# Split maxima turned into rows by two 64-row matmuls, a LayerNorm part on ScalarE, maxima 19 steps ahead

## The chip, the cores and the metric

The kernel runs on one core of a Trainium2 chip. The metric is the device time of one execution in microseconds (us). Before the change three runs took 1256.53, 1258.13 and 1259.32 us; the median is 1258.13. Engine names: PE is TensorE's matmul, PEld its weight load, DVE is VectorE, ACT ScalarE, POOL GpSimd, and SP is SyncE, which issues all the DMAs of this kernel.

## The reference

A pre-LayerNorm transformer block in float32: 2048 positions, width 448, 16 query heads of 28 columns that share one key and one value head, and a gated feed-forward part of 1792 columns.

```
h  = x + Attention(LN(x))      q = 16 heads x 28, k and v one head of 28
       p = softmax(q k^T * 28^-0.5);  (p v, heads side by side) @ wo
out = h + (silu(LN(h) @ w1) * (LN(h) @ w3)) @ w2
LN(x) = (x - mean) / sqrt(var + 1e-5), without gain or bias
```

## The kernel before

To keep float32 accuracy with fast matmuls, a value is split into a high part in the rounded type fp32r and a low part, the value minus the high part, and products are summed over high x high, low x high and high x low.

**Blocks and steps.** The queries are in 4 tiles of 512 (t) and 4 groups of 4 heads (g); one (t, g) is a block, i = 4t + g, 16 blocks. The attention loop (line 559) has 256 steps, 16 per block: step s = 16i + c treats key chunk c of 128 keys for block i. In a step, four `Head`s (line 269) each do two 64-row matmuls (key chunk as weights, QS[i] with 512 queries as the moving side), and ACT takes the exponential from PSUM (line 286). One step later `pv` (line 289) multiplies the exponentials with the values in four matmuls of 128 x 32 tiles, accumulated in a PSUM tile of its own (po).

**Maxima.** The softmax subtracts each row's true maximum. For that the scores are computed a second time, queries as weights and 512 keys as the moving side: a `Unit` (line 218) is one such matmul of 128 queries, 512 keys, one head, and a DVE maximum (line 236) of its 128x512 result. Each step has four units, for the block `AHEAD` = 20 steps on (`a_units`, line 349), so the last unit of block i is in step 16i-5. They come in pairs from heads that sit in the upper and lower 64 rows of QS. At the end of that step `max_done` (line 246) takes the maximum over the key tiles and negates it: nm, 128 queries x 16 columns. In the middle of step 16i-3 `max_rows` turns nm into 16 rows of 128 by one full transpose on PE (line 253), ACT copies the high part (line 255), and `max_low` subtracts it on DVE (line 260); then SP issues 8 DMAs (line 267) that put the rows into row 28 of each 32-row part of QS[i], where the keys' matrix holds ones. Thus the heads of block i, from step 16i on, add the negated maximum by the matmul itself.

**What sets the order.** Every engine executes in the order in which the program text issues: the schedule is manual. `at(s, fn)` (line 519) hangs a function on a step: a whole number is the end of the step, 0.4 and 0.5 its middle, before and after the maxima of the first two units are issued. In even steps the third and fourth head alternate with two units each, with PV between; in odd steps all four heads come first, then two units, PV, two units (lines 585 to 612). PSUM tiles other than po come from seven banks that are handed out as a ring (`bank`, `done`, lines 107 to 114): `bank` takes the one freed longest ago in program order, so a tile waits for the reader of the seventh tile before it.

**Second LayerNorm.** After a tile t is complete, in the blocks that follow, `wo_rows` (line 324) projects it and adds it to X, `ln_stats` and `ln_rstd` take mean, variance and the inverse root (a power on POOL, line 161), `ln_norm` (line 163) normalizes 128x448 on DVE, four per tile, and `ln_tr` transposes. For t = 0 and 1 this is done beside the attention steps (line 545), for t = 2 and 3 in the feed-forward part (line 671).

**Start.** Before the loop come the first LayerNorm, the projections and the splits of the weights (`split_wq`, lines 387 to 392, two of its subtractions on POOL), and, between projection matmuls, the units of block 0 and the first steps of block 1 in pairs (`both`, the list `first`, line 449).

Of the kernel before, what the change touches and what calls it, by code (L numbers as in the profile page):

```python
# [8 lines left out]
F32 = mybir.dt.float32  # L9
F32R = mybir.dt.float32r  # L10
AF = mybir.ActivationFunctionType
ALU = mybir.AluOpType
AX = mybir.AxisListType
# [3 lines left out]
P = 128  # L17
S = 2048
D = 448
# [3 lines left out]
T = 512  # L23
NT = S // T
NQ = T // P
NG = H // 4
NC = S // P
# [1 line left out]
NI = NT * NG  # L29
EPS = 1e-5  # L30
SCALE = DH ** -0.5
AHEAD = 20


@with_exitstack
def block_kernel(
# [13 lines left out]
    ve, se, ge, pe, sy = nc.vector, nc.scalar, nc.gpsimd, nc.tensor, nc.sync  # L50
# [4 lines left out]
    def f(ap):  # L55
        return ap.bitcast(F32)


    keep = ctx.enter_context(tc.tile_pool(name="keep", bufs=1))
    xt_pool = ctx.enter_context(tc.tile_pool(name="xt", bufs=2))  # L60
    ln_pool = ctx.enter_context(tc.tile_pool(name="ln", bufs=2))
    qs_pool = ctx.enter_context(tc.tile_pool(name="qs", bufs=3))
    wk_pool = ctx.enter_context(tc.tile_pool(name="work", bufs=2))
# [3 lines left out]

    X = [keep.tile([P, NQ, D], F32, name=f"X{t}") for t in range(NT)]
    ident = keep.tile([P, P], F32, name="ident")
    pexp = keep.tile([P, NQ], F32, name="pexp")  # L70
    KS = keep.tile([P, S], F32R, name="KS", tag="ks")
    VA = keep.tile([P, NC, 32], F32, name="VA")
# [34 lines left out]
    def bank(name="pb"):  # L107
        k = free.pop(0)
        ps = ps_w.tile([P, T], F32, name=name, tag=f"bank{k}")
        used[id(ps)] = ps, k  # L110
        return ps

    def done(ps):
        free.append(used.pop(id(ps))[1])
# [32 lines left out]
    LN = {}  # L147

    def ln_stats(t, n):
        if n == 0:  # L150
            LN[t] = (ln_pool.tile([P, NQ, 6], F32, name="st"),
                     ln_pool.tile([P, NQ, 2], F32, name="mv"),
                     ln_pool.tile([P, NQ], F32, name="rs"), {})
        st, mv, _, _ = LN[t]
        ve.bn_stats(st[:, n], X[t][:, n])
        ve.bn_aggr(mv[:, n], st[:, n])

    def ln_rstd(t, n0=0, n1=NQ):
        _, mv, rs, _ = LN[t]
        ve.tensor_scalar(rs[:, n0:n1], mv[:, n0:n1, 1], EPS, None, op0=ALU.add)  # L160
        ge.tensor_tensor(rs[:, n0:n1], rs[:, n0:n1], pexp[:, n0:n1], op=ALU.pow)

    def ln_norm(t, n):
        _, mv, rs, xns = LN[t]
        xn = xns[n] = ln_pool.tile([P, 512], F32, name="xn", bufs=4)
        ve.tensor_scalar(xn[:, :D], X[t][:, n], mv[:, n, 0:1], rs[:, n : n + 1],  # L166
                         op0=ALU.subtract, op1=ALU.mult)
        ge.tensor_copy(xn[:, D:], xn[:, 384:D])

    XT = {}  # L170
# [19 lines left out]
        done(last)  # L190


    MR = {}
    QS, MX, NM, PT, PO, WH, WS = {}, {}, {}, {}, {}, {}, {}

    def build_qs(i, ps=None):
        t, g = divmod(i, NG)
        st = wk_pool.tile([P, 2, T], F32R, name="qst")
        if ps is None:
            q = QR[t][:, g]  # L200
            se.activation(st[:, 0], q, AF.Copy)  # L201
            ge.tensor_tensor(st[:, 1], q, f(st[:, 0]), op=ALU.subtract)  # L202
        else:
            se.activation(st[:, 0], ps, AF.Copy)
            ve.tensor_tensor(st[:, 1], ps, f(st[:, 0]), op=ALU.subtract)


        QS[i] = qs_pool.tile([P, 4, T], F32R, name="qs")
        for p in range(2):
            for jj in range(2):  # L210
                for b in range(2):
                    r, j = 64 * jj + 32 * b, 2 * p + jj
                    sy.dma_start(f(QS[i][r : r + 32, 2 * p : 2 * p + 2]), f(st[32 * j : 32 * j + 32]))

    def rows(jj):
        return slice(64 * jj, 64 * jj + 64)

    class Unit:
# [7 lines left out]
        def mm(self):  # L226
            i, n, kt, r = self.i, self.n, self.kt, rows(self.jj)
            if i not in MX:
                MX[i] = wk_pool.tile([P, 16, 4], F32, name="mx")
            self.ps = bank("pa")  # L230
            pe.matmul(self.ps, QS[i][r, 2 * self.p, n * P : (n + 1) * P], KS[r, kt * T : (kt + 1) * T],  # L231
                      start=True, stop=True)

        def red(self):
# [9 lines left out]
            u.red()  # L244

    def max_done(i):
        NM[i] = wk_pool.tile([P, 16], F32, name="nm")
        ve.tensor_reduce(NM[i], MX[i], axis=AX.X, op=ALU.max, negate=True)  # L248

    def max_rows(i):  # L250

        ps = bank()
        pe.transpose(ps[:16, :P], NM[i], ident)  # L253
        mr = wk_pool.tile([16, 2, P], F32R, name="mr")
        se.activation(mr[:, 0], ps[:16, :P], AF.Copy)
        MR[i] = ps, mr

    def max_low(i):
        ps, mr = MR.pop(i)
        ve.tensor_tensor(mr[:, 1], ps[:16, :P], f(mr[:, 0]), op=ALU.subtract)  # L260
        done(ps)
        for k in range(2):
            for jj in range(2):
                r = 64 * jj + 32 * k + 28
                for p in range(2):
                    c = 8 * jj + 4 * p
                    sy.dma_start(f(QS[i][r : r + 1, 2 * p]).rearrange("o (n q) -> o n q", n=NQ), f(mr[c : c + 4, k]))  # L267

    class Head:

# [4 lines left out]
        def mm(self, k):  # L275
            i, c, (p, jj) = self.i, self.c, divmod(self.j, 2)
            if k == 0:
                self.ps = bank()
            r = rows(jj)
            pe.matmul(self.ps, KS[r, c * P : (c + 1) * P], QS[i][r, 2 * p + k], start=(k == 0), stop=(k == 1))  # L280

        def exp(self):
            i, c, (p, jj) = self.i, self.c, divmod(self.j, 2)
# [64 lines left out]

    def a_units(step):

        i, c = divmod(step, NC)
        if i >= NI:
            return None
        p, n = divmod(c // 2, NQ)
        us = [Unit(i, p, n, 2 * (c % 2) + k, jj) for jj in (1, 0) for k in range(2)]
        return us if c % 2 == 0 else [us[0], us[2], us[3], us[1]]


    for n in range(NQ):
        sy.dma_start(X[0][:, n], xv[0][:, n])  # L360
    make_identity(nc, ident)
    ge.memset(pexp, -0.5)

    with tc.tile_pool(name="start", bufs=1) as sp:
# [83 lines left out]

        first = [(both, 0, *divmod(pn, NQ), kt) for kt in range(4) for pn in range(8)]
        first.append((max_done, 0))  # L450
        for c in range(AHEAD - NC):
            first += [(both, 1, *divmod(c // 2, NQ), 2 * (c % 2) + k) for k in range(2)]
        first[-5:-5] = [(max_rows, 0), (max_low, 0)]

        def pairs(n=2):
            while n > 0 and first:
# [62 lines left out]
    def at(s, fn, *args):  # L519
        todo.setdefault(s, []).append((fn, args))  # L520
# [1 line left out]
    for g in range(NG):  # L522
        at(1 + 2 * g, split_wo, g)
    for i in range(1, NI):
        at(NC * i - 5, max_done, i)
        at(NC * i - 2.6, max_rows, i)
        at(NC * i - 2.5, max_low, i)
    for k in range(3, NI):
        at(NC * (k - 2) + 1, build_qs, k)
    LAST = NC * NI  # L530
    for i in range(NI - 1):
        e = NC * (i + 1)
# [3 lines left out]
    for t in range(NT - 1):  # L536
        e = NC * NG * (t + 1)
        for n in range(NQ):
            at(e + 14 + 2 * n, wo_rows, t, n)
            at(e + 14 + 2 * n, ln_stats, t, n)  # L540
        at(e + 22, ln_rstd, t)
        if t == NT - 2:
            continue
        for n in range(NQ):
            at(e + 23 + 2 * n, ln_norm, t, n)
        for c in range(4):
            at(e + 33.5 + 2 * c, lambda t, c: ln_tr(t, c, True), t, c)
    for t in range(NT):
# [5 lines left out]
    def run(s):  # L554
        for fn, args in todo.get(s, []):
            fn(*args)

    prev = None
    for s in range(LAST):
        i, c = divmod(s, NC)  # L560
        au = a_units(s + AHEAD)
        if s in (LAST - 6, LAST - 3):
            WH[0, (s - LAST + 6) // 3] = split_w((s - LAST + 6) // 3)
        if s == LAST - 2:
            WS[0, 0] = split_w2(0)
        hs = [Head(i, c, j) for j in range(4)]

        def pair(a, b):
            for k in range(2):
                a.mm(k)  # L570
                b.mm(k)
            a.exp()
            b.exp()

        def beside(h, us):
            for k in range(2):
                h.mm(k)
                us[k].mm()
            h.exp()

        def red(us):
            for u in us:
                u.red()

        pair(hs[0], hs[1])
        if au and c % 2 == 0:
            beside(hs[2], au[:2])
            run(s + 0.4)
            red(au[:2])
            run(s + 0.5)  # L590
            if prev is not None:
                pv(*prev)
            beside(hs[3], au[2:])
            red(au[2:])
        elif au:
            pair(hs[3], hs[2])
            for u in au[:2]:
                u.mm()
            run(s + 0.4)
            red(au[:2])  # L600
            run(s + 0.5)
            pv(*prev)
            for u in au[2:]:
                u.mm()
            red(au[2:])
        else:
            pair(hs[2], hs[3])
            run(s + 0.4)
            run(s + 0.5)
            pv(*prev)  # L610
        prev = (i, c)
        run(s)
# [120 lines left out]
```

## Time and profile before

| what | value |
|---|---|
| median of three runs | 1258.13 us |
| the profiled execution, its own time | 1257.51 us |
| its span, first to last instruction | 1255.7 us |
| mean granted TensorE clock | 0.997 of 2.4 GHz |
| busy: PE, DVE, ACT, POOL | 98%, 69%, 53%, 26% |
| attention loop, first PV matmul to last | 103.0 to 814.2 us |

In the profile an instruction stands under its source line; "out<-in" are tiles by name, "x8" a count. A wait is put down to the instruction that released it. A window's length is the difference of its two bounds, and a busy share of 1.00 under the clock is 2.4 GHz.

### The profile page before, as it was taken

To read this page: it belongs to the slowest core of one execution; us is meant where nothing else is said; L and a number is where in the kernel's file an instruction comes from. 1 tells how busy PE (TensorE), PEld (TensorE's weight loads), DVE (VectorE), ACT (ScalarE), POOL (GpSimd) and SP (SyncE) were. 2 spreads that over 40 slices of the span, in tenths; PEclk is the share of its full clock that TensorE was granted. 3 is DMA by queue.
4 is the path that set the end of the run, shared out by engine and by line. 5 is a ranking of instruction groups with operands and counts; after the bars stand their busy time and mean duration, and the time that the engine had idled before them with its cause. 6 is when DMAs were issued, how large, how long until landed. Compare 5 with 4: busy or idle time off the path is not lost.

```text
span 1255.7 us, 19960 instructions
## 1 busy us (share of the span) xinstructions
PE 1235.7 (98%) x7596; PEld 768.0 (61%) x7596; DVE 860.8 (69%) x1480; ACT 660.9 (53%) x1255; POOL 324.3 (26%) x240
## 2 busy tenths in 40 slices
PE   6999999999999999999999999999999999999998
PEld 4655444444544444544445543488888888888887
DVE  7998999999898999899998894033333334333333
ACT  3316878887688887688886687921111111211111
POOL 3201011101112101111110110344555445455551
PEclk9999999999999999999999999999999999999999
DMA  6220113110103110112110110023000000000000
GB/s 188 62 45 2 36 32 77 44 25 21 44 2 77 44 40 6 43 24 56 43 45 2 43 28 17 10 79 111 1 30 1 1 1 30 1 1 31 1 1 30
DMA packets 37960, 43.08 MB, mean 34 GB/s; under 512 B 12056, under 2 KB 30680, under 8 KB 37864
## 3 DMA queue, kind: packets, MB, share of 16 engines
q1 hardware_dynamic: 37864, 41.81, 12.8%
q8 instruction: 60, 0.98, 0.3%
q14 instruction: 36, 0.29, 0.1%
HBM read 20.25 MB, written 3.80 MB: 19 GB/s over the span
## 4 chain that ended last, share of the span: by engine, by line
PE 91%; DVE 6%; issue 1%; DMA 1%; POOL 0%; SPq 0%; ACT 0%; POOLq 0%
PE pa L127 23%; PE pb L280 21%; PE po L293 19%; PE pb L641 11%; PE pa L231 9%; DVE mx L236 5%; PE pb L127 4%; PE pa L330 3%; PE pb L179 1%; DMA qs<-mr 0%; PE pb L253 0%; DVE xn L166 0%; DVE nm L248 0%; SPq L267 0%; DMA X<-in_A_x_dram 0%
## 5 line engine op out<-in xcount | busy, mean ns | idle before, releaser
L236 DVE TENSOR_REDUCE mx<-pa 128x1 f32<-128x512 f32 x1024 | 635.9, 682 | 36.3 <-PE pa L231 14.8
L286 ACT ACTIVATE pt<-pb 128x512 f32<-128x512 f32 x1024 | 533.9, 601 | 153.9 <-PE pb L280 118.1
L280 PE MATMUL pb<-qs,KS 64*128 64x512 f32 x2048 | 358.2, 403 | 2.0 <-DMA qs<-mr 2.0
L280 PEld LDWEIGHTS pb<-qs,KS 64*128 64x128 f32 x2048 | 227.5, 185 | 159.8 <-DVE mx L236 80.5
L231 PE MATMUL pa<-KS,qs 64*128 64x512 f32 x1024 | 291.7, 441 | 0.9 <-ACT vt L425 0.9
L293 PE MATMUL po<-pt,VA 128*32 128x512 f32 x2048 | 274.4, 606 | 0.0
L127 PE MATMUL pa<-xh,qs 128*128 128x512 f32 x896 | 235.9, 395 | 0.0
L231 PEld LDWEIGHTS pa<-KS,qs 64*128 64x128 f32 x1024 | 133.7, 184 | 130.8 <-DVE mx L236 86.8
L127 PEld LDWEIGHTS pa<-xh,qs 128*128 128x128 f32 x896 | 167.8, 187 | 38.6 <-issue 0.8
L629 DVE TENSOR_TENSOR pt<-pa,pt 128x512 f32<-128x512 f32 x56 | 38.7, 691 | 222.7 <-PE pa L127 222.7
L641 PE MATMUL pb<-qst,pt 128*128 128x448 f32 x672 | 145.8, 367 | 0.0
L627 ACT ACTIVATE pt<-pa 128x512 f32<-128x512 f32 x56 | 33.5, 598 | 197.6 <-PE pa L127 197.5
L641 PEld LDWEIGHTS pb<-qst,pt 128*128 128x128 f32 x672 | 125.7, 188 | 12.5
L632 ACT ACTIVATE pt<-pt 128x512 fp32r<-128x512 f32 x56 | 35.4, 632 | 152.1 <-DVE pt L629 152.1
L202 POOL TENSOR_TENSOR qst<-QR,qst 128x512 fp32r<-128x512 f32 x15 | 19.3, 1285 | 314.7 <-ACT qst L201 314.7
L127 PE MATMUL pa<-xl,qs 128*128 128x512 f32 x336 | 96.4, 395 | 0.0
L293 PEld LDWEIGHTS po<-pt,VA 128*32 128x32 f32 x2048 | 40.9, 108 | 78.6 <-issue 72.0
L340 POOL TENSOR_TENSOR qs<-QR,qs 128x1024 fp32r<-128x1024 f32 x32 | 76.4, 2388 | 16.2 <-DVE qs L339 16.2
L317 POOL TENSOR_TENSOR OT<-OT,rb 128x512 f32<-128x512 f32 x16 | 20.8, 1298 | 201.3 <-PE pb L280 70.7
L127 PEld LDWEIGHTS pa<-xl,qs 128*128 128x128 f32 x336 | 62.9, 187 | 15.5
L633 DVE TENSOR_TENSOR pt<-pt 128x512 fp32r<-128x512 f32 x56 | 40.8, 728 | 39.1 <-ACT pt L632 39.1
L346 POOL TENSOR_TENSOR qst<-w_wo,qst 128x448 fp32r<-128x448 f32 x24 | 35.3, 1469 | 93.9 <-DVE qst L345 93.9
(80 smaller groups left out, 632.2 us busy)
## 6 DMA issues: line engine op xcount, KB each, us to landing
qs<-qst SPq DMA_DIRECT2D x128, 128.0 KB
rb<-sd SPq DMA_DIRECT2D x64, 64.0 KB
QR<-in_B_w_dram SPq DMA_DIRECT2D x16, 192.0 KB
X<-in_A_x_dram SPq DMA_DIRECT2D x3, 896.0 KB
out_dram<-X SPq DMA_DIRECT2D x3, 896.0 KB
qs<-mr SPq DMA_DIRECT2D x128, 2.0 KB
w<-in_B_w_dram SPq DMA_DIRECT2D x8, 192.0 KB
w_wo<-in_B_w_dram SPq DMA_DIRECT2D x6, 224.0 KB
```

What stands on the lines that cost most here:

```text
L127: pe.matmul(ps, lhs[b][:, cb, lsl], rhs[a][:, ca, rsl], start=(k == 0), stop=(k == len(terms) - 1),)
L231: pe.matmul(self.ps, QS[i][r, 2 * self.p, n * P : (n + 1) * P], KS[r, kt * T : (kt + 1) * T], start=True, stop=True)
L236: ve.tensor_reduce(MX[self.i][:, c, self.kt : self.kt + 1], self.ps, axis=AX.X, op=ALU.max)
L280: pe.matmul(self.ps, KS[r, c * P : (c + 1) * P], QS[i][r, 2 * p + k], start=(k == 0), stop=(k == 1))
L286: se.activation(f(PT[i, c, p][:, jj]), self.ps, AF.Exp, bias=0.0, scale=SCALE)
L293: pe.matmul(PO[i][32 * j : 32 * j + 32], VA[:, c], f(PT[i, c, j // 2][:, j % 2]), start=(c == 0), stop=(c == NC - 1))
L330: pe.matmul(ps, OS[a][:, g, n * P : (n + 1) * P], WO[b][:, g], start=(k == 0), stop=(k == 11))
L340: ge.tensor_tensor(wl, W13[k], f(wh), op=ALU.subtract)
L629: ve.tensor_tensor(sg, ps[1], sg, op=ALU.mult)
L632: se.activation(h[:, 0], sg, AF.Copy)
L633: ve.tensor_tensor(h[:, 1], sg, f(h[:, 0]), op=ALU.subtract)
L641: pe.matmul(Y[t][n][:, :D], hid[a][:, n * P : (n + 1) * P], w2s[:, b, :D], start=(k == 0 and m == 0), stop=(k == NF - 1 and m == 2))
```

## The change

- `AHEAD` is 19, so the last unit of block i is in step 16i-4, and two unit pairs fewer are computed at the start. `max_done` moves to the end of step 16i-4; `max_rows` stays in the middle of step 16i-3.
- `max_done` also splits: ACT copies the high part of nm into columns 0 to 15 of a zeroed 128x128 tile, POOL puts the low part into columns 16 to 31.
- `max_rows` makes two matmuls, one for each half of 64 queries, with the split tile as weights (64 rows, 128 columns) and a 64x64 identity as the moving side; each writes a PSUM tile of its own, and ACT copies 32x64 out of each. `max_low` is gone. Four DMAs of 4 KB replace eight of 2 KB; for that the four slots of QS are reordered.
- `ln_norm` in the attention loop runs on ACT, as scale and bias per row; `ln_rstd` gets two POOL operations of 128x4 for that bias wherever it treats a whole tile.

```diff
@@ -29,7 +29,7 @@
 NI = NT * NG
 EPS = 1e-5
 SCALE = DH ** -0.5
-AHEAD = 20
+AHEAD = 19
 
 
 @with_exitstack
@@ -67,6 +67,8 @@
 
     X = [keep.tile([P, NQ, D], F32, name=f"X{t}") for t in range(NT)]
     ident = keep.tile([P, P], F32, name="ident")
+    turn = keep.tile([P, 64], F32R, name="turn")
+    NEG = [keep.tile([P, P], F32R, name=f"neg{k}") for k in range(2)]
     pexp = keep.tile([P, NQ], F32, name="pexp")
     KS = keep.tile([P, S], F32R, name="KS", tag="ks")
     VA = keep.tile([P, NC, 32], F32, name="VA")
@@ -150,21 +152,27 @@
         if n == 0:
             LN[t] = (ln_pool.tile([P, NQ, 6], F32, name="st"),
                      ln_pool.tile([P, NQ, 2], F32, name="mv"),
-                     ln_pool.tile([P, NQ], F32, name="rs"), {})
-        st, mv, _, _ = LN[t]
+                     ln_pool.tile([P, NQ], F32, name="rs"), {}, ln_pool.tile([P, NQ], F32, name="nb"))
+        st, mv, _, _, _ = LN[t]
         ve.bn_stats(st[:, n], X[t][:, n])
         ve.bn_aggr(mv[:, n], st[:, n])
 
     def ln_rstd(t, n0=0, n1=NQ):
-        _, mv, rs, _ = LN[t]
+        _, mv, rs, _, nb = LN[t]
         ve.tensor_scalar(rs[:, n0:n1], mv[:, n0:n1, 1], EPS, None, op0=ALU.add)
         ge.tensor_tensor(rs[:, n0:n1], rs[:, n0:n1], pexp[:, n0:n1], op=ALU.pow)
-
-    def ln_norm(t, n):
-        _, mv, rs, xns = LN[t]
+        if n1 - n0 == NQ:
+            ge.tensor_tensor(nb, mv[:, :, 0], rs, op=ALU.mult)
+            ge.tensor_scalar(nb, nb, -1.0, None, op0=ALU.mult)
+
+    def ln_norm(t, n, act=False):
+        _, mv, rs, xns, nb = LN[t]
         xn = xns[n] = ln_pool.tile([P, 512], F32, name="xn", bufs=4)
-        ve.tensor_scalar(xn[:, :D], X[t][:, n], mv[:, n, 0:1], rs[:, n : n + 1],
-                         op0=ALU.subtract, op1=ALU.mult)
+        if act:
+            se.activation(xn[:, :D], X[t][:, n], AF.Identity, bias=nb[:, n : n + 1], scale=rs[:, n : n + 1])
+        else:
+            ve.tensor_scalar(xn[:, :D], X[t][:, n], mv[:, n, 0:1], rs[:, n : n + 1],
+                             op0=ALU.subtract, op1=ALU.mult)
         ge.tensor_copy(xn[:, D:], xn[:, 384:D])
 
     XT = {}
@@ -190,8 +198,7 @@
         done(last)
 
 
-    MR = {}
-    QS, MX, NM, PT, PO, WH, WS = {}, {}, {}, {}, {}, {}, {}
+    QS, MX, PT, PO, WH, WS = {}, {}, {}, {}, {}, {}
 
     def build_qs(i, ps=None):
         t, g = divmod(i, NG)
@@ -210,7 +217,7 @@
             for jj in range(2):
                 for b in range(2):
                     r, j = 64 * jj + 32 * b, 2 * p + jj
-                    sy.dma_start(f(QS[i][r : r + 32, 2 * p : 2 * p + 2]), f(st[32 * j : 32 * j + 32]))
+                    sy.dma_start(f(QS[i][r : r + 32, p::2]), f(st[32 * j : 32 * j + 32]))
 
     def rows(jj):
         return slice(64 * jj, 64 * jj + 64)
@@ -228,7 +235,7 @@
             if i not in MX:
                 MX[i] = wk_pool.tile([P, 16, 4], F32, name="mx")
             self.ps = bank("pa")
-            pe.matmul(self.ps, QS[i][r, 2 * self.p, n * P : (n + 1) * P], KS[r, kt * T : (kt + 1) * T],
+            pe.matmul(self.ps, QS[i][r, self.p, n * P : (n + 1) * P], KS[r, kt * T : (kt + 1) * T],
                       start=True, stop=True)
 
         def red(self):
@@ -244,27 +251,25 @@
             u.red()
 
     def max_done(i):
-        NM[i] = wk_pool.tile([P, 16], F32, name="nm")
-        ve.tensor_reduce(NM[i], MX[i], axis=AX.X, op=ALU.max, negate=True)
+
+        nm, neg = wk_pool.tile([P, 16], F32, name="nm"), NEG[i % 2]
+        ve.tensor_reduce(nm, MX[i], axis=AX.X, op=ALU.max, negate=True)
+        se.activation(neg[:, :16], nm, AF.Copy)
+        ge.tensor_tensor(neg[:, 16:32], nm, f(neg[:, :16]), op=ALU.subtract)
 
     def max_rows(i):
 
-        ps = bank()
-        pe.transpose(ps[:16, :P], NM[i], ident)
-        mr = wk_pool.tile([16, 2, P], F32R, name="mr")
-        se.activation(mr[:, 0], ps[:16, :P], AF.Copy)
-        MR[i] = ps, mr
-
-    def max_low(i):
-        ps, mr = MR.pop(i)
-        ve.tensor_tensor(mr[:, 1], ps[:16, :P], f(mr[:, 0]), op=ALU.subtract)
-        done(ps)
+        mr, ps = wk_pool.tile([32, P], F32R, name="mr"), [bank(), bank()]
+        for jj in range(2):
+            r = rows(jj)
+            pe.matmul(ps[jj][:, :64], NEG[i % 2][r], turn[r], start=True, stop=True)
+        for jj in range(2):
+            se.activation(mr[:, rows(jj)], ps[jj][:32, :64], AF.Copy)
+            done(ps[jj])
         for k in range(2):
             for jj in range(2):
-                r = 64 * jj + 32 * k + 28
-                for p in range(2):
-                    c = 8 * jj + 4 * p
-                    sy.dma_start(f(QS[i][r : r + 1, 2 * p]).rearrange("o (n q) -> o n q", n=NQ), f(mr[c : c + 4, k]))
+                r, c = 64 * jj + 32 * k + 28, 16 * k + 8 * jj
+                sy.dma_start(f(QS[i][r : r + 1, :2]).rearrange("o p (n q) -> o (p n) q", n=NQ), f(mr[c : c + 8]))
 
     class Head:
 
@@ -277,7 +282,7 @@
             if k == 0:
                 self.ps = bank()
             r = rows(jj)
-            pe.matmul(self.ps, KS[r, c * P : (c + 1) * P], QS[i][r, 2 * p + k], start=(k == 0), stop=(k == 1))
+            pe.matmul(self.ps, KS[r, c * P : (c + 1) * P], QS[i][r, 2 * k + p], start=(k == 0), stop=(k == 1))
 
         def exp(self):
             i, c, (p, jj) = self.i, self.c, divmod(self.j, 2)
@@ -348,17 +353,21 @@
 
     def a_units(step):
 
-        i, c = divmod(step, NC)
+        i, c = divmod(step + AHEAD, NC)
         if i >= NI:
             return None
         p, n = divmod(c // 2, NQ)
         us = [Unit(i, p, n, 2 * (c % 2) + k, jj) for jj in (1, 0) for k in range(2)]
-        return us if c % 2 == 0 else [us[0], us[2], us[3], us[1]]
+        return us if step % 2 == 0 else [us[0], us[2], us[3], us[1]]
 
 
     for n in range(NQ):
         sy.dma_start(X[0][:, n], xv[0][:, n])
     make_identity(nc, ident)
+    for jj in range(2):
+        ge.tensor_copy(turn[rows(jj)], ident[rows(jj), rows(jj)])
+    for w in NEG:
+        ge.memset(f(w), 0.0)
     ge.memset(pexp, -0.5)
 
     with tc.tile_pool(name="start", bufs=1) as sp:
@@ -450,7 +459,7 @@
         first.append((max_done, 0))
         for c in range(AHEAD - NC):
             first += [(both, 1, *divmod(c // 2, NQ), 2 * (c % 2) + k) for k in range(2)]
-        first[-5:-5] = [(max_rows, 0), (max_low, 0)]
+        first[-3:-3] = [(max_rows, 0)]
 
         def pairs(n=2):
             while n > 0 and first:
@@ -522,9 +531,8 @@
     for g in range(NG):
         at(1 + 2 * g, split_wo, g)
     for i in range(1, NI):
-        at(NC * i - 5, max_done, i)
-        at(NC * i - 2.6, max_rows, i)
-        at(NC * i - 2.5, max_low, i)
+        at(NC * i - 4, max_done, i)
+        at(NC * i - 2.5, max_rows, i)
     for k in range(3, NI):
         at(NC * (k - 2) + 1, build_qs, k)
     LAST = NC * NI
@@ -542,7 +550,7 @@
         if t == NT - 2:
             continue
         for n in range(NQ):
-            at(e + 23 + 2 * n, ln_norm, t, n)
+            at(e + 23 + 2 * n, ln_norm, t, n, True)
         for c in range(4):
             at(e + 33.5 + 2 * c, lambda t, c: ln_tr(t, c, True), t, c)
     for t in range(NT):
@@ -558,7 +566,7 @@
     prev = None
     for s in range(LAST):
         i, c = divmod(s, NC)
-        au = a_units(s + AHEAD)
+        au = a_units(s)
         if s in (LAST - 6, LAST - 3):
             WH[0, (s - LAST + 6) // 3] = split_w((s - LAST + 6) // 3)
         if s == LAST - 2:
```

## Rows read from the trace of the kernel before

**Rows 1.** The page: busy time of TensorE over the span, and the chain's shares.
```profile
PE 1235.7 (98%) x7596; PEld 768.0 (61%) x7596; DVE 860.8 (69%) x1480; ACT 660.9 (53%) x1255; POOL 324.3 (26%) x240
...
PE 91%; DVE 6%; issue 1%; DMA 1%; POOL 0%; SPq 0%; ACT 0%; POOLq 0%
```

**Rows 2.** Windows: stretch, length, busy (count) of PE, PEld, DVE, ACT, POOL, clock, DMA.
```profile
481.79:484.63 2.84, 2.84 (x25) 1.42 (x23) 2.84 (x5) 2.35 (x6) 0.00 (x0) 1.00 0.00 0
...
484.63:486.99 2.36, 2.36 (x21) 1.07 (x19) 2.13 (x5) 1.82 (x5) 0.00 (x0) 1.00 0.00 0
...
486.99:490.35 3.36, 3.25 (x26) 1.70 (x24) 3.33 (x7) 2.87 (x7) 0.00 (x0) 1.00 0.02 5
...
490.35:492.70 2.35, 2.35 (x19) 1.01 (x18) 2.03 (x5) 1.39 (x5) 0.00 (x0) 1.00 0.01 3
```

**Rows 3.** Timeline, 486.9 to 492.7 us: start, duration, engine, line, [idle before <-releaser].
```profile
487.48 0.22 DVE L248 TENSOR_REDUCE nm<-mx 128x16 f32<-128x64 f32 x1
...
487.62 3.67 DVE L236 TENSOR_REDUCE mx<-pa 128x1 f32<-128x512 f32 x6
...
491.47 0.28 DVE L260 TENSOR_TENSOR mr<-pb,mr 16x128 fp32r<-16x128 f32 x1 [0.19 <-ACT mr L255]
...
488.75 2.59 ACT L286 ACTIVATE pt<-pb 128x512 f32<-128x512 f32 x5 [0.49 <-PE pa L231]
...
491.19 0.25 ACT L255 ACTIVATE mr<-pb 16x128 fp32r<-16x128 f32 x1
...
489.47 0.56 PE L231 MATMUL pa<-KS,qs 64*128 64x512 f32 x2
...
490.35 1.06 PE L293 MATMUL po<-pt,VA 128*32 128x512 f32 x8
...
490.14 0.09 PEld L253 LDWEIGHTS pb<-ident,nm 128*16 128x16 f32 x1 [0.41 <-DVE mx L236]
```

**Rows 4.** Windows: intervals 15, into a block's first heads: first, last, sum of nine.
```profile
140.64:143.26 2.62, 2.62 (x20) 1.18 (x18) 2.39 (x5) 2.00 (x6) 0.00 (x0) 1.00 0.01 2
...
733.67:736.37 2.70, 2.70 (x21) 1.19 (x19) 2.47 (x5) 2.00 (x6) 0.00 (x0) 1.00 0.01 2
...
sum 25.10, PE 24.68 PEld 10.68 DVE 22.88 ACT 18.09 POOL 0.00; mean PE 2.74 PEld 1.19 DVE 2.54 ACT 2.01 POOL 0.00
```

**Rows 5.** Windows: intervals that hold a DVE normalization of the second LayerNorm.
```profile
344.96:348.11 3.15, 3.15 (x24) 1.66 (x22) 3.15 (x6) 2.66 (x6) 0.24 (x1) 1.00 0.00 0
...
355.97:359.76 3.79, 3.68 (x25) 1.59 (x23) 3.75 (x8) 3.30 (x8) 0.24 (x1) 1.00 0.00 0
```

**Rows 6.** Windows around the last block's start, and a later plain step.
```profile
767.57:769.89 2.32, 2.32 (x19) 0.92 (x17) 0.68 (x2) 2.27 (x6) 0.00 (x0) 1.00 0.00 0
...
774.16:779.09 4.93, 3.40 (x19) 1.14 (x17) 0.00 (x0) 2.99 (x7) 0.00 (x0) 0.87 0.01 3
...
779.09:782.17 3.08, 3.08 (x17) 0.96 (x16) 0.00 (x0) 1.75 (x4) 0.00 (x0) 0.66 0.00 0
...
796.05:798.18 2.13, 2.13 (x18) 0.83 (x20) 0.00 (x0) 2.07 (x5) 2.13 (x2) 1.00 0.00 0
```

**Rows 7.** Timeline there: SP's eight issues, and the weights that waited.
```profile
771.59 5.20 SPq L267 DMA_DIRECT2D qs<-mr  x8
...
777.25 0.30 PEld L280 LDWEIGHTS pb<-qs,KS 64*128 64x128 f32 x4 [1.07 <-DMA qs<-mr]
```

**Rows 8.** Lines by form, GpSimd: shapes, count, busy us, mean ns, idle before.
```profile
L202 POOL TENSOR_TENSOR qst<-QR,qst 128x512 fp32r<-128x512 f32 x15 | 19.3, 1285 | 314.7 <-ACT qst L201 314.7
...
L385 POOL TENSOR_TENSOR WKV<-wkv_r,WKV 128x384 fp32r<-128x384 f32 x1 | 1.0, 1001 | 0.5 <-ACT WKV L384 0.5
```

**Rows 9.** Timeline of the start: GpSimd, the weights waiting for it, one unit pair.
```profile
16.81 1.33 POOL L161 TENSOR_TENSOR rs<-rs,pexp 128x4 f32<-128x4 f32 x1 [5.66 <-DVE rs L160]
...
19.28 0.19 PEld L127 LDWEIGHTS pb<-xh,OS 128*128 128x128 f32 x1 [2.67 <-POOL OS L392]
...
95.92 0.50 PE L231 MATMUL pa<-KS,qs 64*128 64x512 f32 x2
```

## The prediction

> **What bounds the kernel now.** I read the page first: TensorE (PE) is busy in 98% of the span and carries 91% of the chain of waits [rows 1]. A busy PE is not a PE at its peak, so I then cut the attention loop into intervals. An interval runs from the weighted-value product (PV, line 293) of one step to that of the next, and I number it by its step in the block, 0 to 15. A plain even interval takes 2.84 us and a plain odd one 2.36 [rows 2], the first two windows: 5.20 for two steps. PE is busy all of it, VectorE (DVE) 4.97, ScalarE (ACT) 4.17, GpSimd (POOL) nothing, the clock is 1.00. The reader is to see that PE sets the pace in a plain step: DVE work that goes is worth nothing there unless PE waited for it. So I looked for intervals longer than plain ones; the change can only win or lose in these.
>
> Four kinds exist. Interval 12, where the maxima are turned into rows, takes 3.36 instead of 2.84 [rows 2]: 0.52 too long, in nearly every block. Interval 15, into the first heads of the next block, which need the rows by DMA, is too long in nine blocks: 25.10 in all [rows 4], less 9 x 2.36 = 3.9. The intervals with a DVE normalization are 3.15 instead of 2.84, and where it meets the maxima 3.79 instead of 3.36 [rows 5]. Around the last block four intervals lose several us [rows 6].
>
> The timeline of interval 12 says why it is long [rows 3]. The transpose's weights (line 253) start at 490.14, waiting for DVE. Seven PSUM banks go round as a ring, so its bank is that of the seventh tile before it: the last unit of the step before. That unit's max is the fourth of the six that start at 487.62, 0.60 apart ((3.67 - 0.68) / 5), so it ends at 487.62 + 1.80 + 0.68 = 490.10. PV follows 0.21 later, at 490.35. The negated maxima themselves (nm, line 248) were done at 487.70 and made nobody wait: they had a whole step.
>
> **The change, part by part.** *Maxima 19 ahead, the split on ACT and POOL: interval 12.* With 19 steps the last unit of a block is in step 16i-4, not 16i-5, so nm now comes behind that fourth max, while PE needs the split maxima where the transpose stood, half a step on. Walked through on [rows 3]:
> - Without nm in front of them the four maxima end some 0.25 earlier (nm's 0.22 and its hand-over): 489.85. nm then runs from 489.88 to 490.10.
> - ACT copies the high part. Its queue is in order: behind the fourth step-12 exponential (488.75 to 489.35) and ahead of step 13's first, which now starts at 489.27. The copy of 16 columns was never run here; the 16x128 copy of line 255 took 0.25, a 512 column exponential takes 0.60. Bounds 0.1 to 0.65, taken 0.20: 490.13 to 490.33.
> - POOL subtracts, 128x16. Subtractions of 512 and 384 columns take 1285 and 1001 ns [rows 8], 2.2 ns a column and 0.15 for none: 0.19 for 16. Bounds 0.1 and 1.3 (the 512 column row). Ready about 490.60.
> - The first small matmul could load at 490.60. The second takes the next bank of the ring, that of step 13's first head. Its exponential now starts behind the ACT copy, at 490.28, and ends at 490.88. So the second matmul goes at 490.93, and PV 0.2 later as behind the transpose: 491.14 instead of 490.35. The two matmuls are priced at that 0.2, bounds 0.05 and 0.5 (two unit matmuls after a change of tile, [rows 9]).
>
> Interval 12 grows by 0.79, to about 4.15. In interval 13 the next even step's first head takes the bank of step 13's last head, whose exponential ends at 490.28 + 3 x 0.49 + 0.60 = 492.35, against 491.14 + 1.10 = 492.24 when PE wants it: 0.14 more. Queued behind the waiting ACT copy are those four exponentials; behind the waiting matmul PV and the next two units, so DVE idles. PE has no slack in which to recover either. In 14 blocks 14 x 0.93 = +13.0.
>
> *What goes from DVE.* The subtraction of line 260 (0.28 and 0.19 idle) lies in an interval of 2.35, no longer than plain [rows 2]: worth nothing.
>
> *Four row DMAs for eight.* SP issues eight in 5.20, 0.65 each [rows 7]; the weights that wait for the seventh, issued at 771.59 + 6 x 0.65 = 775.5, start at 777.25: about 1.7 after its issue. Four issues from 492.6 (the two ACT copies behind step 13's exponentials) land by 492.6 + 1.95 + 1.7 = 496.3; the heads that want them come at 491.14 + 2.50 + 2.84 + 1.1 = 497.6. The excess of interval 15 goes: -3.9. What is late next is nothing, with 1.3 to spare.
>
> *LayerNorm on ACT.* Eight DVE normalizations go. Six cost 0.31 each, two 0.43 each [rows 5]: -2.7. ACT has 0.54 free in an odd interval [rows 2], and 448 columns take less than the exponential's 0.60 for 512: hidden. If that cover is gone it costs the difference. The Trainium skill (ScalarE: Activation LUTs, What ACT_TABLE_LOAD costs) gives 186 ns plus 0.833 ns a column and 93 ns more for each operand that is a pointer to a column; here scale and bias both are, so by it the operation would be 0.75, at most 0.2 over the gap eight times: an estimate of 1.6 less gain. No row here has an activation with two such operands.
>
> *Last block.* The five intervals from 767.57 to 782.17 took 14.60, with PE waiting for the rows and the clock at 0.87 and 0.66 [rows 6]. Now step 16i-4 has units, and no units follow: PV comes at about 490.9 on the scale above, an interval of 3.9; then 2.13, 2.13, 2.13 and some 2.6 (the output copy on ACT): 12.9, since the four DMAs just make it. -1.7, the extra step of units included.
>
> *Start.* Two unit pairs fewer. One took up to 0.50 on PE [rows 9], one rode beside another: between 0 and 1.0, taken -0.65. Against this POOL gets two 128x4 operations between the power at 16.81 and the weight splits at 18.11, for which PE waited 2.67 [rows 9]: about 0.2 each, bounds 0.1 and 1.3, +0.4. Together -0.25.
>
> *Rows of QS reordered, padding, the ident copies:* the loads of QS come twelve steps before use, and POOL is idle then; nothing.
>
> Sum: 13.0 - 3.9 - 2.7 - 1.7 - 0.25 = +4.5. The profiled execution took 1257.5 (span 1255.7, and 1.8 around it), so 1262.0; it lies 0.6 under the median of 1258.1.
>
> **The rivals.** *A, the wait is hidden.* If what makes interval 12 long is mostly the transpose's own change of tile, two matmuls in the units' 64-row tiles bring it to about 2.95, -0.4 in 14 blocks, nothing in interval 13, and the last block gains 3.5: -5.7 - 3.9 - 2.7 - 3.5 - 0.25 = -16, 1241. In favour: PEld waits 0.41 there and the transpose alone stands in 16-column tiles. Against: the bank's max ended at 490.10 and the transpose went 0.04 later, so a wait, not the tile, set it; and nm now comes after that same max. It decides if the split maxima are ready by 489.9, 0.7 sooner than I find. The Trainium skill (TensorEngine Tiling (Array Packing), Key Properties) says that changing the tiling mode drains the engine, which speaks for this rival; the 0.21 from the transpose to PV is all that the rows leave for it. *A', half of the wait hidden* (DVE further ahead than walked): +0.25 in 14 blocks, -8.5 for the rest: -5, 1252.5.
>
> *B, POOL is dear.* If the small subtraction costs 1.0 instead of 0.19, as the 128x4 power with 1.33 suggests [rows 9], PV slips to 491.6, interval 13 is plain: 14 x 1.25 - 8.5 = +9, 1266.5. If the clock fell after the new waits as it did in the last block, it would be more: an interval at 0.66 took 3.08 [rows 6], some 0.9 over plain; in 14 blocks +12 beside my +4.5, 1274. Against the latter: two idles of 0.78 and 0.75 led to that fall, mine are near 0.7 alone.
>
> *C, no change that can be told.* The chain costs 0.6 a block, not 0.93 (a shorter copy, interval 13 untouched): 8.4 - 8.5 = 0, 1257.5.
>
> **How the numbers follow.** A measurement of this kernel can tell about 0.2%, 2.5 us. My forecast, 1259 to 1265, has 0.54, of which 0.06 falls within 0.2%; B 0.14; C 0.12; A 0.08; A' 0.12. So faster 0.20, same 0.18, slower 0.62. The likeliest has 1262.0, own range 1259 to 1265. From 1250 to 1270 takes in A', C, the forecast and the first of B, and leaves out A and the clock's case (0.04).
>
> **What would show it.** Interval 12 at 4.1 in the changed trace, ACT idle for 0.7 before the 128x16 copy with DVE's nm as releaser, small matmuls waiting for ACT or POOL, interval 13 at 2.5, interval 15 at 2.36, normalization intervals at 2.84, no DMA wait at the last block. If interval 12 is at or under 3.4, the forecast is wrong, and the time is near 1245.

## Result, and the profile after

The changed kernel takes 1263.52 us (median of 6 runs, 1262.65 to 1264.20) against 1257.94 (6 runs) of the kernel before on the same chip: ratio 1.0043, 95% interval 1.0030 to 1.0056, 5.6 us slower. The forecast was 1262.0, own range 1259 to 1265. The profiled execution took 1262.77, with a span of 1260.8 instead of 1255.7.

The page of the changed kernel, busy time by engine and the chain of waits by engine:

```profile
PE 1231.3 (98%) x7612; PEld 769.3 (61%) x7612; DVE 852.1 (68%) x1456; ACT 668.3 (53%) x1295; POOL 333.5 (26%) x274
...
PE 83%; issue 8%; DVE 5%; POOL 2%; SPq 1%; DMA 1%; ACT 1%; POOLq 0%; DVEq 0%; ACTq 0%
```

PE is busy for 4.4 us less than in [rows 1] in a span that is 5.1 longer: it waits more. The windows of the changed kernel, columns as in [rows 2], show where. In order: intervals 12 and 13 of the block of [rows 2], an interval 15, the first and the second normalization interval of a tile, and around the last block's start intervals 12, 13, 15 and 0.

```profile
490.43:494.61 4.18, 3.38 (x26) 1.83 (x24) 4.07 (x8) 2.83 (x7) 0.22 (x1) 1.00 0.01 4
494.61:496.97 2.36, 2.36 (x19) 1.01 (x18) 1.02 (x3) 1.66 (x6) 0.00 (x0) 1.00 0.00 0
...
227.55:229.91 2.36, 2.36 (x21) 1.02 (x19) 2.13 (x5) 1.81 (x5) 0.00 (x0) 1.00 0.00 0
348.02:351.13 3.11, 3.11 (x25) 1.54 (x23) 2.85 (x5) 3.04 (x7) 0.24 (x1) 1.00 0.00 0
353.48:356.32 2.84, 2.84 (x25) 1.39 (x23) 2.84 (x5) 2.35 (x6) 0.00 (x0) 1.00 0.02 6
...
773.71:777.72 4.01, 2.89 (x25) 1.40 (x23) 3.07 (x6) 2.67 (x7) 0.22 (x1) 1.00 0.00 0
777.72:779.84 2.12, 2.12 (x18) 0.82 (x17) 0.00 (x0) 1.84 (x6) 0.00 (x0) 1.00 0.00 0
781.97:784.45 2.48, 2.48 (x18) 1.06 (x16) 0.00 (x0) 2.26 (x6) 0.00 (x0) 1.00 0.02 3
784.45:786.58 2.13, 2.13 (x18) 0.83 (x18) 0.00 (x0) 2.13 (x6) 0.00 (x0) 1.00 0.00 0
```

Interval 12 went from 3.36 to 4.18, with PE idle for 0.80 of it; interval 13 is plain; interval 15 fell to plain; the normalization intervals fell to plain but for the first of each tile; the last block's wait [rows 6] is nearly gone, and the clock stays at 1.00 there. The timeline of that interval 12, which answers to [rows 3] (start, duration, engine, line):

```profile
493.39 0.22 DVE L256 TENSOR_REDUCE nm<-mx 128x16 f32<-128x64 f32 x1
...
493.64 0.22 ACT L257 ACTIVATE neg<-nm 128x16 fp32r<-128x16 f32 x1 [0.86 <-DVE nm L256]
493.76 2.04 ACT L291 ACTIVATE pt<-pb 128x512 f32<-128x512 f32 x4
...
493.93 0.22 POOL L258 TENSOR_TENSOR neg<-nm,neg 128x16 fp32r<-128x16 f32 x1 [13.31 <-ACT neg L257]
...
494.20 0.37 PEld L265 LDWEIGHTS pb<-turn,neg 64*128 64x128 f32 x2 [1.12 <-POOL neg L258]
494.61 0.16 PEld L298 LDWEIGHTS po<-pt,VA 128*32 128x32 f32 x8
...
496.14 0.69 DVE L243 TENSOR_REDUCE mx<-pa 128x1 f32<-128x512 f32 x1 [1.34 <-PE pa L238]
```

It is the walk of the prediction, link by link: nm behind the last maximum, then ACT, which has stood idle for 0.86 with step 13's exponentials queued behind the copy, then POOL, then the weights, which waited; and DVE, which everyone waited for, idles for 1.34 afterwards because the next units come late.

Two more lines of the changed kernel are needed below: the normalization on ACT, from the view by form (count, busy us, mean ns, idle before), and POOL's weight splits at the start, from the timeline.

```profile
L172 ACT ACTIVATE xn<-X,nb,rs 128x448 f32<-128x448 f32 x8 | 6.1, 768 | 0.7 <-POOL nb L166 0.7
```

```profile
18.81 2.58 POOL L401 TENSOR_TENSOR OS<-OT,OS 128x448 fp32r<-128x448 f32 x2
```

### The profile page after: what moved, and what is told of

It reads as the page before. It is cut to its first block, busy times and chain, and to the rows that moved or that the text cites. A ratio compares the mean times of both kernels' runs of the same rounds, so it can differ in the third digit from the quotient of the medians.

```text
span 1260.8 us, 19897 instructions
## 1 busy us (share of the span) xinstructions
PE 1231.3 (98%) x7612; PEld 769.3 (61%) x7612; DVE 852.1 (68%) x1456; ACT 668.3 (53%) x1295; POOL 333.5 (26%) x274
## 4 chain that ended last, share of the span: by engine, by line
PE 83%; issue 8%; DVE 5%; POOL 2%; SPq 1%; DMA 1%; ACT 1%; POOLq 0%; DVEq 0%; ACTq 0%
PE pa L129 23%; PE pb L285 18%; PE po L298 16%; PE pb L649 11%; PE pa L238 6%; PE pb L129 4%; DVE mx L243 3%; PE pa L335 3%; PE pb L187 1%; SPq L220 1%; PE pb L265 1%; POOL OS L327 0%; DVE st L157 0%; DMA rb<-sd 0%; POOL OT L322 0%
## 5 line engine op out<-in xcount | busy, mean ns | idle before, releaser
L285 PE MATMUL pb<-qs,KS 64*128 64x512 f32 x2048 | 354.6, 401 | 0.0
L258 POOL TENSOR_TENSOR neg<-nm,neg 128x16 fp32r<-128x16 f32 x16 | 3.5, 222 | 216.3 <-ACT neg L257 216.3
```

## The experiments

All ratios are against the kernel before, run beside. Line numbers in a fence are of the kernel it is from; the cuts of code show the lines that matter, and "..." stands for lines left out. "The loop" is the time from the first PV matmul to the first of the PV in step 255, the last step; it is 709.0 in the kernel before and 713.3 in the changed one.

**The normalization on ACT alone.** The kernel before with only this part; of its edit the one line that moves the operation:

```diff
-            at(e + 23 + 2 * n, ln_norm, t, n)
+            at(e + 23 + 2 * n, ln_norm, t, n, True)
```

> The kernel before with the second LayerNorm's normalization (t = 0 and 1) on ACT, and nothing else of the change. The changed kernel's trace: six of the eight normalization intervals fall by 0.31 to 0.43 us, the first of each tile (3.15) stays. Theory of parts that add up: -2.0 in the loop, +0.4 or nothing at the start (two POOL operations before the weight splits), so 1256.0 to 1256.5, ratio 0.9987. Rival, the operations with two column pointers (0.76 us) delay the exponentials and with them PE: no gain, ratio 1.000 or over.

Measured: 1258.39 (11 runs), ratio 1.0003 (0.9994 to 1.0011): no change. The rival's result, but not for its reason. The normalization intervals did fall, and part of the gain was given back at the next block's first heads, whose row DMAs were already late. The first two windows are a normalization interval (3.15 before) and interval 14 of the first such block, the third the same block's interval 15, which was a plain 2.35 before:

```profile
352.47:355.31 2.84, 2.84 (x24) 1.40 (x22) 2.84 (x5) 2.35 (x6) 0.00 (x0) 1.00 0.03 6
363.38:366.23 2.85, 2.85 (x25) 1.39 (x23) 2.85 (x5) 2.36 (x6) 0.00 (x0) 1.00 0.02 4
366.23:368.93 2.70, 2.70 (x20) 1.18 (x19) 2.48 (x5) 1.99 (x6) 0.00 (x0) 1.00 0.01 2
```

Of 2.1 won in six intervals of two tiles 0.7 went this way. In the profiled execution the loop is still 1.8 shorter than before; but the first PV comes 2.1 later, at 105.0, and the part behind the loop is 0.6 longer. The start varies by as much between executions (last section), so what the two POOL operations add to it is not shown by the total.

**Four row DMAs alone.** The kernel before with QS reordered, and:

```diff
-                for p in range(2):
-                    c = 8 * jj + 4 * p
-                    sy.dma_start(f(QS[i][r : r + 1, 2 * p])..., f(mr[c : c + 4, k]))
+                c = 8 * jj
+                sy.dma_start(f(QS[i][r : r + 1, :2])..., f(mr[c : c + 8, k]))
```

> The kernel before with the four slots of QS reordered and four row DMAs of 4 KB in place of eight of 2 KB, and nothing else. Theory: intervals 15 fall to 2.36 in all blocks (-3.9 in nine) and the wait at the last block, its two long intervals and the fall of the clock go (-3.4): about 1250.5, ratio 0.994. Interval 12 stays at 3.36. Rival, the maxima in rows are late by themselves and not by the number of issues: intervals 15 stay at 2.6 to 3.1 and the time at 1258.

Measured: 1251.68, ratio 0.9950 (0.9935 to 0.9965). At the last block, where [rows 6] has 4.93 and 3.08 with the clock at 0.87 and 0.66, and in an interval 12:

```profile
485.27:488.65 3.38, 3.27 (x26) 1.72 (x24) 3.35 (x7) 2.89 (x7) 0.00 (x0) 1.00 0.02 5
771.12:773.81 2.69, 2.58 (x19) 1.06 (x17) 0.00 (x0) 2.27 (x6) 0.00 (x0) 1.00 0.01 3
773.81:775.94 2.13, 2.13 (x18) 0.83 (x17) 0.00 (x0) 2.13 (x6) 0.00 (x0) 1.00 0.00 0
```

The number of issues on SP was the cause of the late rows, and this part alone is worth 6 us (7.5 in the loop of the profiled execution, whose first PV came 1.2 later than in the kernel before). So the rest of the change costs about 12.

**The split on DVE.** The changed kernel, with

```diff
-        se.activation(neg[:, :16], nm, AF.Copy)
-        ge.tensor_tensor(neg[:, 16:32], nm, f(neg[:, :16]), op=ALU.subtract)
+        ve.tensor_copy(neg[:, :16], nm)
+        ve.tensor_tensor(neg[:, 16:32], nm, f(neg[:, :16]), op=ALU.subtract)
```

> The changed kernel with both halves of the split on DVE (two 128x16 operations) in place of the copy on ACT and the subtraction on POOL. ACT's queue no longer holds an operation that waits for DVE; the chain behind the last maximum stays in being, nm and two more DVE operations. Theory, the chain behind the last maximum sets interval 12: the small matmuls start about 0.1 sooner and the second no longer waits for step 13's first exponential, interval 12 goes from 4.19 to about 3.9: -0.3 in 15 blocks, -4.5, 1259. Rival, ACT's queue alone is the cost: interval 12 at 3.2 or less, 1248. Rival, the two matmuls are dear by themselves: 4.19 and 1263.5 as in the changed kernel.

Measured: 1258.10 (10 runs), ratio 1.0006 (0.9997 to 1.0015). Interval 12 is 3.81; the chain on DVE, and the weights that wait for it:

```profile
490.83 0.22 DVE L256 TENSOR_REDUCE nm<-mx 128x16 f32<-128x64 f32 x1
491.08 0.17 DVE L257 CAST neg<-nm 128x16 fp32r<-128x16 f32 x1
491.29 0.17 DVE L258 TENSOR_TENSOR neg<-nm,neg 128x16 fp32r<-128x16 f32 x1
...
491.52 0.18 PEld L265 LDWEIGHTS pb<-turn,neg 64*128 64x128 f32 x2 [0.91 <-DVE neg L258]
```

The chain behind the last maximum is the main part of the wait. The way over ACT and POOL had added 0.37 of 4.18: from the end of nm to the first weights it is 0.47 here and 0.60 there, and both weights load at once here, where the second had come 0.19 later, behind the exponential that ACT's copy had held up.

**Twenty steps ahead again.** The changed kernel, with the split at the end of step 16i-5:

```diff
-AHEAD = 19
+AHEAD = 20
...
-        at(NC * i - 4, max_done, i)
+        at(NC * i - 5, max_done, i)
```

> The changed kernel with the maxima 20 steps ahead again and max_done, with its split on ACT and POOL, at the end of step 16i-5: the split has a whole step more before PE needs it. Theory, only the lead time was short: interval 12 at 3.2 to 3.36 (the bank of the seventh tile before), -0.9 in 15 blocks, 1250. Rival, the copy in ACT's queue costs wherever it stands right behind a last maximum: it would now hold up the exponentials of step 12 by about 1.0 us (they are due 0.8 before nm ends), PE would wait for their banks, interval 11 or 12 together would be some 0.7 to 1.0 over plain, and the time 1257 to 1263.

Measured: 1262.91, ratio 1.0041 (1.0028 to 1.0055): the rival. The split is ready at 492.90, two us before PE loads it, and interval 12 is still 4.03. On ACT the copy waits 1.69 for nm, ahead of exponentials that are due, and PE then waits three times for the bank of one:

```profile
492.39 0.22 ACT L257 ACTIVATE neg<-nm 128x16 fp32r<-128x16 f32 x1 [1.69 <-DVE nm L256]
492.51 2.04 ACT L291 ACTIVATE pt<-pb 128x512 f32<-128x512 f32 x4
```

```profile
493.14 0.18 PEld L238 LDWEIGHTS pa<-KS,qs 64*128 64x128 f32 x1 [0.28 <-ACT pt L291]
493.62 0.18 PEld L285 LDWEIGHTS pb<-qs,KS 64*128 64x128 f32 x1 [0.30 <-ACT pt L291]
494.11 0.75 PEld L285 LDWEIGHTS pb<-qs,KS 64*128 64x128 f32 x7 [0.30 <-ACT pt L291]
```

So lead time is not enough: two things are wrong, the lead and the copy's place in ACT's queue.

**The small matmuls behind PV.** The changed kernel, with a hook behind PV in odd steps:

```diff
-        at(NC * i - 2.5, max_rows, i)
+        at(NC * i - 3 + 0.6, max_rows, i)
...
             pv(*prev)
+            run(s + 0.6)
```

> The changed kernel with the two small matmuls and what follows them moved behind PV in step 16i-3 (one PV, 1.0 us, later); the split stays on ACT and POOL at the end of step 16i-4. Theory: PE no longer waits for the split, since PV now covers the chain, so interval 12 falls from 4.19 to 2.85; but the copy still holds the four exponentials of step 13 by about 0.8, and the two unit matmuls behind the small ones, and the next step's first head, take the banks of those exponentials: interval 13 grows from 2.36 to about 3.2. Together -0.5 in 15 blocks: 1256. Rival, ACT's queue has slack enough: interval 13 at 2.5, 1246. Rival, PE waits as long as before, only behind PV: 1263.

Measured: 1262.97, ratio 1.0038 (1.0024 to 1.0052): no gain. Interval 12 is 2.91, as the theory has it, but interval 13 is 3.64, not 3.2. The small matmuls start at once behind PV now, and behind them PE's weights wait three times 0.30 for an exponential of step 13. The theory had a wait of 0.8 on a plain interval; it left out that the small matmuls take time of their own: without the waits this interval is 2.61, as the next kernel shows.

```profile
495.66 0.18 PEld L238 LDWEIGHTS pa<-KS,qs 64*128 64x128 f32 x1 [0.30 <-ACT pt L291]
496.15 0.18 PEld L238 LDWEIGHTS pa<-KS,qs 64*128 64x128 f32 x1 [0.30 <-ACT pt L291]
...
496.63 0.53 PEld L285 LDWEIGHTS pb<-qs,KS 64*128 64x128 f32 x5 [0.30 <-ACT pt L291]
```

```profile
491.21:494.12 2.91, 2.91 (x25) 1.47 (x23) 2.85 (x5) 1.87 (x4) 0.00 (x0) 1.00 0.00 0
494.12:497.76 3.64, 3.45 (x21) 1.44 (x20) 2.79 (x6) 2.63 (x8) 0.22 (x1) 1.00 0.00 0
...
sum 6.55, PE 6.36 PEld 2.90 DVE 5.65 ACT 4.50 POOL 0.22; mean PE 3.18 PEld 1.45 DVE 2.82 ACT 2.25 POOL 0.11
```

The two intervals have the same sum as in the changed kernel, 4.18 + 2.36 = 6.54: moving the matmuls alone moves PE's wait and does not shorten it, since the exponentials come as late as before.

**Both together.** The split on DVE and the small matmuls behind PV.

> The changed kernel with the split on DVE and the small matmuls behind PV. Theory: no exponential waits for a maximum, the split ends under PV (it ended 0.3 after PE was ready for PV in the kernel with the split alone on DVE): interval 12 at 2.85, interval 13 at about 2.5 for the two matmuls, together -0.8 in 15 blocks against the split on DVE alone, 1246, ratio 0.990. Rival, the two more DVE operations make DVE the later engine: interval 14 longer, 1250 or over.

Measured: 1248.58, ratio 0.9925 (0.9910 to 0.9939). Each edit alone left the kernel at 1258 and 1263; together they remove both waits, 2.91 + 2.61 = 5.52:

```profile
483.25:486.16 2.91, 2.91 (x25) 1.47 (x23) 2.88 (x6) 2.42 (x6) 0.00 (x0) 1.00 0.00 0
486.16:488.77 2.61, 2.61 (x22) 1.12 (x21) 2.54 (x7) 1.94 (x6) 0.00 (x0) 1.00 0.00 0
```

**The copy in ACT's gap.** The kernel with 20 steps, but nm at the end of step 16i-5, its split on ACT and POOL in the middle of step 16i-4, and the small matmuls behind PV.

```diff
         at(NC * i - 5, max_done, i)
+        at(NC * i - 3.5, max_split, i)
+        at(NC * i - 3 + 0.6, max_rows, i)
```

> The changed kernel with the maxima 20 steps ahead, nm at the end of step 16i-5, the split on ACT and POOL in the middle of step 16i-4, where ACT is idle for 0.5 us, and the small matmuls behind PV. The same operations on the same engines as in the kernel with 20 steps alone (1262.9), whose copy stood ahead of exponentials that were due. Theory, the place in ACT's queue is the cost: interval 12 at 2.85, interval 13 at 2.5, 1246. Rival, ACT has no room for the copies wherever they stand: 1255 or over.

Measured: 1247.50, ratio 0.9917 (0.9902 to 0.9932). Intervals 12 and 13 are 3.06 and 2.48, 5.54 together. Here ACT does the same copy of 0.23 and waits for nothing before it:

```profile
482.54 1.57 ACT L297 ACTIVATE pt<-pb 128x512 f32<-128x512 f32 x3 [0.55 <-PE pb L291]
483.98 0.23 ACT L263 ACTIVATE neg<-nm 128x16 fp32r<-128x16 f32 x1
```

**Two more edits on top of both together.** The bias only where ACT uses it, and `ln_rstd` a step earlier.

```diff
-        if n1 - n0 == NQ:
+        if nbias:
...
-        at(e + 22, ln_rstd, t)
+        at(e + 21, ln_rstd, t, 0, NQ, True)
```

> The split on DVE, the small matmuls behind PV, and two more edits: the bias of the normalization is computed only where ACT uses it (two POOL operations less before the weight splits at the start, -0.4), and ln_rstd stands one step earlier, so that the first normalization of each tile doesn't wait for POOL (that interval falls from 3.11 to 2.85, -0.3 twice). Theory: 1.0 under the kernel without these two, about 1245. Rival, the start is set by something else: no gain there, 1245.5.

Measured: 1245.15 (1244.81 to 1246.18), ratio 0.9900 (0.9885 to 0.9915): the fastest, 12.8 under the kernel before, and 3.4 under the kernel without the two edits, not 1.0. The first normalization interval is plain now (2.84), which is 0.5 in two tiles. The rest lies before the first PV, at 101.2 instead of 104.3, and is not the two POOL operations alone, as the last section tells: these delay the weight splits by 0.7 (18.81 against 18.11), and the clock at the start differs.

**The old maxima with the rest.** The kernel before with the four DMAs, the normalization on ACT and those two edits.

> The kernel before (maxima 20 ahead, the transpose on PE, the low part on DVE) with the parts of the change that have nothing to do with how the maxima are split and turned: four row DMAs, and the normalization on ACT with its bias computed only where it is used and ln_rstd one step earlier. Theory, the other parts add up once the DMAs no longer bind: the four DMAs measured -6.1, the eight normalization intervals give 6 x 0.31 and 2 x 0.43, -2.7, and intervals 15 do not grow this time as they did with the normalization alone: 1249, ratio 0.993; interval 12 stays at 3.36. Then the maxima part, placed well (1245.2), is worth 3 to 4, and as the change places it (1263.5) it costs 14. Rival, the normalization gives nothing here either: 1251.7.

Measured: 1248.16 (1246.37 to 1249.66), ratio 0.9921 (0.9907 to 0.9934). Interval 12 is at 3.38, as before. The medians would make the maxima part worth 3.0 at its best place (1248.16 less 1245.15), but the five runs of this kernel lie 3.3 apart. The profiled executions of the two kernels tell more, since the clock is 1.00 in both, start and loop. Their loops, the fastest kernel's first:

```profile
101.25:798.39 697.14, 696.81 (x5214) 333.97 (x5213) 613.22 (x1050) 558.14 (x1098) 91.14 (x90) 1.00 0.14 34
```

```profile
101.64:800.18 698.54, 696.79 (x5195) 334.89 (x5194) 610.26 (x1031) 556.20 (x1083) 91.10 (x90) 1.00 0.14 34
```

PE is busy for the same 696.8 in both. The maxima part is worth 1.4 in the loop at its best place; where the change puts it, it costs about 14 (713.3 less 698.5, and less the 0.5 that `ln_rstd`'s place is worth). Against the kernel with four DMAs alone, whose loop is 701.5, this one is 3.0 shorter, 2.8 of it in the eight normalization intervals: with the DMAs late the normalization gave 1.8.

## Why the prediction was right, and where not

- *Interval 12, +0.79 in 14 blocks:* measured 0.82. nm ended 3.18 behind the PV that opens the interval (3.11 was walked to); ACT's copy took 0.22 (0.20 was taken), POOL's subtraction 0.22 (0.19). The second matmul's weights came 0.19 behind the first's, with the end of the exponential that started behind the copy. The kernel with the split on DVE shows the chain, the one with 20 steps the queue. Either alone makes interval 12 long: 3.81 and 4.03.
- *Interval 13, +0.14 in 14 blocks, 2.0 in all:* failed; 2.36, nothing. The bank did come late: the two waiting weight loads of the next step's heads start at 495.85 instead of 0.10 behind the units' at 495.61. But the first matmul behind PV needs 0.34 before the next one streams (495.61 to 495.95), and a load that comes 0.24 behind it is still in time. The walk took the start of a weight load for that of a matmul.
- *DVE's subtraction, worth nothing:* right; interval 13 has 1.02 of DVE work instead of 2.03 [rows 2] and the same length, though maxima of units have moved behind it too.
- *Four DMAs, -3.9:* the nine intervals fell by 3.8. The kernel with this part alone confirms the cause.
- *LayerNorm on ACT, -2.7:* measured -2.2. Six of eight intervals fell by the 0.31 or 0.43 taken; the first of each tile stayed at 3.11, as its ACT operation starts behind POOL's bias. The operation takes 0.77, not under 0.60; where it started on time its interval is plain all the same. By the Trainium skill's price (ScalarE: Activation LUTs, What ACT_TABLE_LOAD costs) the prediction's estimate was 0.75, and the trace agrees with its 0.77.
- *Last block, -1.7:* measured -1.7 (+1.7 in interval 12, -2.4 in 15, -1.0 in 0). The wait was not all gone: interval 15 is 2.48 instead of 2.13, since the second of two heads that else start together came 0.40 later (782.96 and 783.36); the 2.6 forecast for interval 0 did not come (2.13) and makes up for it.
- *Start, -0.25:* +0.05 at the first PV. POOL's splits start at 18.81 instead of 18.11 [rows 9], +0.7 where 0.4 was taken.
- *Left over, 1.2:* intervals 4 are 0.06 to 0.10 longer in nine blocks, 0.6 in all. The 0.06 shows in every kernel with 19 steps ahead and in none with 20. The part behind the loop is 0.6 longer; it is so with the normalization alone too, and 0.3 with the DMAs alone. Why, stays open for both.

The sum is right in part by luck. It was +4.5, and the span grew by 5.1; but the 2.0 of interval 13 never came, and without them the forecast is 1260.0. What filled their place are small misses the other way: 0.4 in interval 12, 0.5 in the normalization, 0.3 at the start, and the 1.2 left over.

The rival in which the transpose's change of tile was the cost is refuted as a forecast: interval 12 did not fall. Placed behind PV and with a split that waits for nobody, the two intervals are 0.2 under those of before (5.52 against 3.36 + 2.35); which part of that is the tile and which the ring's bank was not taken apart. The rival of a dear POOL is refuted by its 0.22, and the fall of the clock by the 1.00 in all these windows.

## What to carry to other kernels

Behind the last piece of a reduction, count every hand-over to the consumer as a wait of its own, and put the consumer far enough behind: here three operations of 0.22 and the hand-overs between them, 0.8 us from the start of nm to the first weights, needed one PV of cover. An operation that waits for another engine costs its own queue as well: look at what stands behind it, and put it where that engine is idle anyway. And a gain in one part can be eaten in part by the next late transfer: of 2.1 us won by the normalization 0.7 were, until the DMAs were on time.

## What the runs showed of the hardware

The start is not the same in each execution. The granted clock between 16 and 30 us was 0.88 in the profiled runs of the kernel before and of the changed one, 0.76 with the normalization alone and 1.00 in the fastest kernel; with it the first PV came at 103.0, 103.0, 105.0 and 101.2. The kernel with the DMAs alone, whose edit touches nothing there, had 0.76 and 104.2. These windows are of the normalization alone and of the fastest kernel:

```profile
16.00:30.00 14.00, 10.51 (x42) 8.07 (x41) 11.01 (x20) 3.91 (x8) 5.44 (x9) 0.76 0.45 127
```

```profile
16.00:30.00 14.00, 11.04 (x57) 8.36 (x56) 12.17 (x26) 4.74 (x9) 6.04 (x8) 1.00 0.48 134
```

PE has waited there for POOL's weight splits, 2.67 in [rows 9] and 3.47 with the normalization alone, where POOL has two more operations; behind these waits the clock was at its lower level (1.2 GHz) for a stretch. But the fastest kernel waits as long as the kernel before, and its clock stays at 1.00:

```profile
19.30 0.19 PEld L129 LDWEIGHTS pb<-xh,OS 128*128 128x128 f32 x1 [2.64 <-POOL OS L401]
```

So the wait alone does not decide it; what does, stays open. Differences of 1 to 3 us between two medians may come from the start alone: 21 runs of the kernel before went from 1256.10 to 1259.24, the shortest at a mean granted clock of 0.999 and the longest at 0.995. The waits of 0.8 in interval 12, 14 of them, left the clock at 1.00.
